# Linear attention and a token mixer in one kernel: the whole work list reordered, more value products on GpSimd

## The chip, the cores and the metric

The kernel runs on one core of one Trainium2 chip. The core has five engines that run their own instruction queues and meet only at semaphores: TensorE (PE in the profile; its weight loads are PEld), VectorE (DVE), ScalarE (ACT), GpSimd (POOL) and SyncE (SP), which here issues all transfers. Tiles lie in SBUF (128 partitions); matrix products land in PSUM (8 banks). The metric is the device time of one execution in microseconds (us), as the median of several runs.

## The reference

Inputs are q, k and v of shape (8 batches, 8 heads, 576 positions, 64 values) in float32, and three weight matrices. The first half is linear attention with position weights:

```python
theta = np.pi / 2.0 * pos / S
def phi(x, c, s):
    r = np.maximum(x, 0.0)
    return np.concatenate([r * c, r * s], axis=-1)
q_p = phi(q, cos_w, sin_w); k_p = phi(k, cos_w, sin_w)
kv = np.einsum('bhsf,bhsd->bhfd', k_p, v)
z = np.sum(k_p, axis=2)
num = np.einsum('bhsf,bhfd->bhsd', q_p, kv)
den = np.einsum('bhsf,bhf->bhs', q_p, z)[..., None] + 1e-06
```

num / den, with the heads side by side, is x of shape (8, 576, 512). The second half mixes tokens: wq = x @ w_q and wk = x @ w_k (512 to 64), W = wq wk^T / 8, mixed = W x, and the result is relu(mixed) @ w_out, of shape (8, 576, 512) in float32.

## The kernel before

The work is cut into 16 groups H of four heads (two for each batch b = H // 2), 8 batches, and 36 row tiles of the output. One string, ORDER, lists every step of the kernel as a short word, and a loop at the end of the kernel function turns the words into instructions one by one. A word is a kind, an index, an optional a or b (one half of a group), @A, @V or @G for ScalarE, VectorE or GpSimd, and :n for the PSUM bank or the slot of the output ring. Since each engine runs its own instructions in the order in which they were issued, ORDER fixes the queue of every engine; between engines only data and buffers decide. The scheduling is manual: nothing reorders the steps.

For a group H the steps are:

- LK, LQ, LV (line 145): half loads of k, q and v, 288 KB each, issued by SyncE into a ring of five float32 buffers (NRAW). LW loads weights, ST (line 519) stores a row tile.
- RK and RQ (lines 203 and 205): relu of k and q, float32 to bf16, on ScalarE, VectorE or GpSimd.
- The value products: v times the position weights vtab, twice as wide as v. Either CV casts v to bf16 and VS multiplies on VectorE (line 234), or VG multiplies on GpSimd straight from the float32 v (line 248). Both write v2, which has two buffers (NV2), so group H needs KV of group H - 2 done.
- KV (lines 275 and 285): k^T times v2 on TensorE; KE evicts it. For groups in KV_WIDE the product is taken in a wide form with 18 matmuls, else in 36 small ones.
- QT: transposes of q on TensorE, wide (line 295, 9 of 128 by 128) for groups in QT_WIDE, narrow (line 301, 18 of 64 by 64) else. QM (lines 316 and 320) multiplies the position weights onto them on VectorE, in two instructions for the wide form and one for the narrow one.
- N (line 340): numerators and denominators on TensorE, one step for each half group g = 2H, 2H + 1. For g in EPS_PE a small product adds the epsilon on TensorE (line 348); else EP adds it (lines 357 and 359). RC takes the reciprocal (line 378), RJ the same for two half groups at once (line 381). X multiplies (line 393) and writes x.
- XT or XR transposes x on TensorE (lines 406 and 419), XE evicts it.

For a batch: WK, WQ, KX (lines 439, 452, 466) with evictions KW, QW, XK and copies across partitions XA and XB; four MX (line 489) with ME (relu, lines 500 and 502). For each row tile: WO, four products with w_out (line 509), OE (eviction), ST (store). CW casts weights; the words that begin with T build tables and constants.

In the order before, stores stand among the last third of the loads in SyncE's queue; a store there waits until its row tile is evicted, and the loads behind it wait too.

The selection of one step's form, and the two ways to the products:

```python
def VS(H, ps, eng, part):
    V.tensor_mul(v2_b[H % NV2][:, part, :, :, 0:D],
        vb_b[H % NPREP][:, part].unsqueeze(3).to_broadcast([P, n, C, 2, D]), ...)
def VG(H, ps, eng, part):
        G.tensor_mul(dst[:, part, :, :, 0:D],
            s[:, part].unsqueeze(3).to_broadcast([P, n, C, 2, D]), ...)
```

Of the kernel before, what the change touches and what calls it, by code (L numbers as in the profile page):

```python
# [26 lines left out]
LK1b TB TI LQ1a LQ0a TK LV1b TZ LV1a LK1a LQ1b TQ LQ0b LK0a RQ1a@G LV0a TW TV LV0b LK0b CV1@A LV3a
LV3b VS1b RQ1b@A LQ3b VS1a T2 QT1:0 LQ3a RK1a@A RK1b@V RQ0@V LK3b KV1:2 QM1 LK3a QT0:4 KE1@A CV0@G
LV2b RK0@A LW1 N2:2 VS0 N3:0 LQ2a LK2a VG3 QM0 KV0:6 LW0 KE0@A LV2a RC3 EP2@A X3 RQ3@A N0:6 N1:4
LQ2b RC2 EP0@V EP1@V X2 RK3@A LK2b QT3:0 RC0 XT1:2 LV5b X0 LV5a XE1@A RC1 X1 VG2b KV3:6 QM3 LK5b  # L30
# [1 line left out]
RC6 LQ4a KX0:4 X6 RK2@A QT2:2 RC7 X7 CV5@A KV2:0 LK7a XK0@V LV4a QM2 XB0@G QW0@A XT3:6 LV4b KE2@A
RK5@A LK4a VS5a N5:0 WU5:2 LK4b N4:2 VS5b XE3@A RQ5@G LV7a EP5@V KV5:4 RC5 RC4 X5 XA0@A LV7b X4
QT5:6 KE5@A RQ4@G LQ7b MX0:0 QM5 XR2:2 ME0@A LQ7a QT4:4 XE2@A LQ6a N10:0 QM4 MX1:6 CV4@G LK7b EP10@A
ME1@A WK1:2 LV6b WQ1:3 RC10 KW1@A VS4 RK4@A LQ6b KX1:2 MX2:6 LW2 N11:4 XK1@V QW1@A ME2@A EP11@V
KV4:2 LK6b RC11 XA1@G X10 CV7a@A CV7b@G LK6a X11 MX5:6 MX4:0 KE4@A RQ7b@G LV6a RQ7a@A VS7 N8:2 N9:4
ME5@A LV8a ME4@A QT7:6 RK7@G LW3 EP8@V EP9@V RJ4 RQ6a@A XT5:0 X8 LW4 XB1@G XE5@A X9 KV7:2 LW5 RQ6b@G
QM7 LQ8b VG6b MX6:4 KE7@A XT4:0 LQ9b ME6@A MX7:2 XE4@V QT6:6 LV8b ME7@A N15:4 QM6 RK6a@A LQ8a MX3:2
N14:0 CV6a@G EP15@A RK6b@A WK2:6 LV9b ME3@A VS6a WQ2:7 LK8a KW2@A RC14 KV6:2 RC15 QW2@A LQ9a X14
CV8a@G KX2:7 LV9a KE6@A CW4@G X15 CW2@A N13:2 LK9a CW3@A CW5@V N12:0 EP13@V XR7:4 XK2@V LK8b WO8:6  # L40
RC13 XA2@A X13 EP12@A CV8b@G LK9b XE7@A WO2:7 RC12 VS8 LV11a WO7:2 CV9b@A RQ8a@G X12 OE8:0@A MX8:4
WO6:3 RQ8b@A RK8a@G LQ13a ME8@V OE7:1@A LQ11b XR6:0 RQ9a@G LQ10a WO1:6 CV9a@A XE6@V RQ9b@G LK11b
OE2:2@A WO4:2 LK11a VS9 OE6:3@A LQ11a RK8b@A QT9:0 RK9a@G OE1:4@A WK3:3 LV11b QM9 QT8:4 RK9b@G KW3@A
# [1 line left out]
WQ3:6 RC16 LQ10b KX3:7 X16 QW3@A MX10:0 LV10a XK3@A N17:4 ME10@A N19:2 RK11@V N18:6 LV10b EP19@A
WO11:0 EP17@V RQ11@A LQ12a RC17 EP18@V X17 WO5:1 VG11b OE11:6@V WO10:4 OE5:5@A RC19 RC18 ST11 X18
WO9:5 LK12a X19 LK10b QT11:6 LQ13b OE9:7@A RQ10@G LV12b KV11:2 XA3@A QM11 XR8:0 LK12b KE11@A XR9:6
VG10a XE8@A QT10:2 LQ12b XE9@V WO0:5 QM10 OE10:8@A MX13:0 OE0:6@A MX12:6 N22:2 WO12:4 RQ13a@G ME12@V
EP22@A LV15a XB3@A ME13@A LV13a RC22 VG10b WK4:5 X22 LQ14b LV14b MX14:0 KW4@A N23:6 ME14@V LQ14a
MX15:2 EP23@A KX4:5 RK10@A LV13b WQ4:0 XK4@V RQ13b@G RC23 WO3:1 ME15@A X23 XA4@G XB4@A QW4@A RQ12b@G  # L50
KV10:2 OE3:9@V RQ12a@A QT13:6 OE12:10@A VG12 MX18:0 WO14:5 QM13 KE10@A ST12 ME18@A LK13b XR11:2
OE14:11@A LK13a MX16:0 N21:6 XE11@V ME16@A LV14a N20:4 EP21@A EP20@V RK12@A QT12:0 RJ10 X21 WO16:2
RQ14b@A X20 WO13:3 QM12 VG13 XR10:4 OE13:10@A MX19:6 KV12:0 ME19@A ST13 WO17:3 OE16:12@A LK15b
KE12@V XE10@V LK14b MX17:0 LK14a OE17:13@A N25:6 ME17@V N24:4 LV15b RQ14a@A WK5:3 ST2 EP25@V EP24@V
RK13@A RJ12 QT14:0 X24 WO21:2 KW5@A X25 CV14a@G KV13:4 OE21:10@A QM14 CV14b@A WQ5:3 ST21 KE13@A
KX5:2 LQ15b VS14 LQ15a XR12:4 XK5@A N27:0 ST3 XE12@A N26:6 LK15a RK14a@G WO20:2 RC26 EP27@V RC27
XA5@G RK14b@A X27 WO19:4 XB5@G QW5@A VG15b X26 KV14:0 OE19:2@A MX21:6 KE14@A MX23:4 WO18:3 ME21@V
ME23@A OE20:10@V XR13:4 RQ15a@G MX22:6 RQ15b@V MX20:0 ST20 ME22@A WO15:2 VG15a ST17 XE13@V ME20@A
ST8 N28:6 OE18:9@V OE15:14@A ST9 N29:0 EP28@A QT15:4 RK15@A EP29@V RC28 WK6:3 RC29 X29 WO25:2 KW6@A
QM15 WQ6:3 OE25:15@A KV15:0 X28 QW6@A ST25 ST7 KX6:3 KE15@A ST15 N31:0 ST18 XR14:6 EP31@V N30:4 ST0  # L60
XE14@V WO23:2 EP30@A ST10 XK6@A RJ15 ST16 X30 XA6@G WO24:3 ST5 OE23:7@A XB6@G X31 WO26:2 OE24:0@A
ST14 XR15:0 ST6 MX25:4 MX27:6 XE15@V ME25@A WO22:3 ST23 ME27@V ST1 WK7:0 OE26:9@V ST24 MX24:6 KW7@A
MX26:4 WQ7:1 ME24@A ME26@V ST19 KX7:0 OE22:8@V ST26 WO28:2 XK7@A QW7@V ST22 XA7@G WO27:3 OE28:11@A
XB7@G ST28 MX31:0 MX28:4 MX30:6 ME31@V ME28@A WO29:2 ME30@A OE27:7@V MX29:4 OE29:4@V WO30:0 ME29@A
ST27 ST29 WO32:1 OE30:2@V WO33:4 ST30 OE32:9@V WO34:0 ST32 OE33:8@A WO35:1 ST33 OE34:7@V WO31:4 ST34
OE35:4@A ST35 OE31:2@A ST31
"""


# [1 line left out]
def kernel(  # L71
# [135 lines left out]
    def cast(eng, dst, s):  # L207
        if eng is A:
            A.copy(dst, s)  # L209
        elif eng is G:  # L210
            G.tensor_scalar(dst, s, 1.0, 1.0, op0=ALU.mult, op1=ALU.mult)  # L211
        else:
            V.tensor_copy(dst, s)  # L213
# [98 lines left out]
    def QM(H, ps, eng):
        if H in QT_WIDE:
            q_t = qt_wide(place["QT", H]).rearrange("p c (r d) -> p r c d", r=2)
            for r in range(2):
                V.tensor_mul(  # L316
                    qm_b[H % NQM][:, :, r, 0:C, :],
                    q_t[:, r].unsqueeze(1).to_broadcast([P, 2, C, H2]), qtab)
# [13 lines left out]
    def N(g, ps, eng):  # L332
# [3 lines left out]
        for u in range(SC):  # L336
            for s in range(2):
                for pr in range(2):
                    a = slice(H2 * pr, H2 * pr + H2)
                    nc.tensor.matmul(  # L340
                        nv[:, pr, u, :], qm_b[H % NQM][a, s, r, 2 * u:2 * u + 2, :],
                        kv_b[H % 2][a, r, pr if H in KV_WIDE else 0, s, 0:D + 1],
                        start=(u == 0 and s == 0),
                        stop=(u == SC - 1 and s == 1 and g not in EPS_PE))
# [254 lines left out]
```

## Time and profile before

| | |
|---|---|
| median of 3 runs | 120.03 us (119.75 to 120.36) |
| span of the profiled execution | 117.9 us, 4967 instructions (it is listed by its span alone) |
| busy in the span | PE 96.3, PEld 65.3, DVE 91.0, ACT 82.7, POOL 64.8 us |
| granted TensorE clock | 0.997 on the mean |
| moved by DMA | 39.38 MB, mean 334 GB/s |

The span runs from the first to the last instruction on the core. Busy time is the union of an engine's instructions. The rest of the runs' time lies around the span. The share of busy time is an average; the stretches of ten microseconds that are shown further down tell more.

### The profile page before, as it was taken

The page shows a single profiled execution, that of the slowest core. Times are in us where ns is not written, and L with a number is a line of the kernel's source. Part 1 is how long each engine was busy: PE and PEld are TensorE (multiplying, and loading weights), DVE is VectorE, ACT ScalarE, POOL GpSimd, SP SyncE. Part 2 cuts the span into 40 slices and gives each one's busy share as a digit, 9 for nine tenths or more (in the row PEclk, how much of TensorE's full clock was granted, in tenths as well). Part 3 has the DMA queues.
Part 4 walks back from the last instruction along what each step waited for, and adds up shares of the span by engine and source line. Part 5 has one row for each costly group of instructions (what it writes and reads, how often), then busy time and mean ns, then how long its engine had stood idle before and what let it go on. Part 6 is the DMA issues. An engine that isn't in the chain of part 4 may idle for free.

```text
span 117.9 us, 4967 instructions
## 1 busy us (share of the span) xinstructions
PE 96.3 (82%) x2109; PEld 65.3 (55%) x2109; DVE 91.0 (77%) x163; ACT 82.7 (70%) x146; POOL 64.8 (55%) x66
## 2 busy tenths in 40 slices
...
GB/s 95 353 389 408 393 363 351 391 389 396 385 393 389 391 385 387 389 395 384 387 381 341 271 317 379 274 253 215 299 285 321 171 205 268 402 343 402 340 306 172
DMA packets 20662, 39.38 MB, mean 334 GB/s; under 512 B 3232, under 2 KB 3232, under 8 KB 20640
## 3 DMA queue, kind: packets, MB, share of 16 engines
...
q8 instruction: 16, 0.26, 1.0%
...
## 4 chain that ended last, share of the span: by engine, by line
PE 46%; DMA 25%; DVE 9%; SPq 8%; ACT 4%; issue 3%; POOL 2%; POOLq 0%; DVEq 0%
PE ps L509 23%; DMA kraw<-in_k_dram 11%; DMA vraw<-in_v_dram 9%; SPq L145 8%; DMA qraw<-in_q_dram 5%; DVE qm L316 5%; PE ps L340 4%; PE ps L452 3%; PE ps L466 3%; PE ps L489 3%; PE ps L439 3%; PE ps L285 3%; PE ps L419 2%; PE ps L295 2%; POOL rq L205 2%
## 5 line engine op out<-in xcount | busy, mean ns | idle before, releaser
L248 POOL TENSOR_TENSOR v<-vraw,vtab 128x1152 bf16<-128x1152 f32 (+1 forms) x12 | 35.6, 2976 | 4.5 <-DVE qm L316 2.5
L509 PE MATMUL ps<-wow,mix 128*128 128x512 bf16 x144 | 34.6, 380 | 0.0
L393 DVE TENSOR_TENSOR x<-ps,rec 128x640 bf16<-128x640 f32 x32 | 25.4, 816 | 0.7
L209 ACT COPY o<-ps 128x512 f32<-128x512 f32 x25 | 14.6, 590 | 10.5 <-PE ps L509 9.2
L316 DVE TENSOR_TENSOR qm<-ps,qtab 128x1152 bf16<-128x1152 bf16 x28 | 19.7, 749 | 1.3 <-PE ps L295 1.2
L509 PEld LDWEIGHTS <-mix 128*128 128x128 bf16 x144 | 12.5, 98 | 14.5 <-issue 1.7
L295 PE MATMUL ps<-ident,rq 128*128 128x128 bf16 x126 | 10.3, 232 | 10.9 <-ACT rq L203 10.0
L234 DVE TENSOR_TENSOR v<-vb,vtab 128x2304 bf16<-128x2304 bf16 (+1 forms) x11 | 12.0, 1110 | 7.5 <-ACT vb L209 6.7
L500 ACT ACTIVATE mix<-ps 128x576 bf16<-128x576 f32 x23 | 14.5, 651 | 2.5 <-PE ps L489 2.3
L340 PE MATMUL ps<-kvs,qm 64*128 64x65 bf16 x640 | 14.0, 193 | 2.8 <-DVE qm L316 1.8
L340 PEld LDWEIGHTS <-qm 64*128 64x128 bf16 x640 | 12.6, 96 | 4.9 <-issue 3.3
L295 PEld LDWEIGHTS <-rq 128*128 128x128 bf16 x126 | 8.2, 104 | 12.5 <-issue 9.9
L203 ACT ACTIVATE rk<-kraw 128x1152 bf16<-128x1152 f32 (+1 forms) x14 | 13.9, 995 | 0.5 <-DMA kraw<-in_k_dram 0.3
L211 POOL TENSOR_SCALAR kx<-kx 64x256 bf16<-64x256 bf16 x10 | 4.0, 400 | 15.8 <-ACT kx L209 10.1
L205 POOL TENSOR_SCALAR rq<-qraw 128x576 bf16<-128x576 f32 (+1 forms) x13 | 10.1, 776 | 4.4 <-ACT rk L203 2.6
L211 POOL TENSOR_SCALAR vb<-vraw 128x576 bf16<-128x576 f32 (+1 forms) x7 | 5.7, 809 | 10.8 <-DMA vraw<-in_v_dram 9.5
L285 PE MATMUL ps<-v,rk 64*64 64x130 bf16 x432 | 9.1, 228 | 1.9 <-ACT mix L500 0.7
L209 ACT CAST kvs<-ps 128x260 bf16<-128x260 f32 (+1 forms) x15 | 6.5, 436 | 5.1 <-PE ps L285 3.8
L285 PEld LDWEIGHTS <-rk 64*64 64x64 bf16 x432 | 7.5, 112 | 4.3 <-ACT mix L500 1.3
L502 DVE TENSOR_SCALAR mix<-ps 128x576 bf16<-128x576 f32 x9 | 6.8, 753 | 3.3 <-PE ps L489 3.1
L213 DVE COPY xT<-ps 128x1280 bf16<-128x1280 bf16 (+1 forms) x9 | 7.3, 813 | 2.2 <-PE ps L419 2.0
L203 ACT ACTIVATE rq<-qraw 128x576 bf16<-128x576 f32 (+1 forms) x10 | 8.3, 830 | 0.9 <-DMA qraw<-in_q_dram 0.8
...
## 6 DMA issues: line engine op xcount, KB each, us to landing
...
```

What stands on the lines that cost most here:

```text
L203: A.activation(dst, s, AF.Relu)
L205: eng.tensor_scalar(dst, s, FMAX, 0.0, op0=ALU.min, op1=ALU.max)
L209: A.copy(dst, s)
L234: V.tensor_mul(v2_b[H % NV2][:, part, :, :, 0:D], vb_b[H % NPREP][:, part].unsqueeze(3).to_broadcast([P, n, C, 2, D]), vtab.unsqueeze(1).t ...
L248: G.tensor_mul(dst[:, part, :, :, 0:D], s[:, part].unsqueeze(3).to_broadcast([P, n, C, 2, D]), vtab.unsqueeze(1).to_broadcast([P, n, C, 2, ...
L285: nc.tensor.matmul(kv_v[o, r, :], rk_of(H)[a, pr, c, :], v2_b[H % NV2][a, pr, c, :, 0:D + 1], start=(c == 0), stop=(c == C - 1))
L295: nc.tensor.transpose(qt_v[:, c, :], rq_b[H % NPREP][:, c, :, :], ident)
L316: V.tensor_mul(qm_b[H % NQM][:, :, r, 0:C, :], q_t[:, r].unsqueeze(1).to_broadcast([P, 2, C, H2]), qtab)
L340: nc.tensor.matmul(nv[:, pr, u, :], qm_b[H % NQM][a, s, r, 2 * u:2 * u + 2, :], kv_b[H % 2][a, r, pr if H in KV_WIDE else 0, s, 0:D + 1], ...
L393: V.tensor_tensor(x_b[b % NX][:, :, 4 * h:4 * h + 4, :].rearrange("p u (w r) d -> p r w u d", r=2)[:, r], nv[:, :, :, 0:D], rec(g).to_broa ...
L500: A.activation(dst, s, AF.Relu, scale=scale_moe)
L509: nc.tensor.matmul(o, mix_b[bp % 2][:, m, rt * P:(rt + 1) * P], wow[:, m, :], start=(m == 0), stop=(m == NDM - 1))
```

## The change

ORDER is written anew from end to end, and four selections change. What can be counted in the two orders:

| | before | after |
|---|---|---|
| value products on GpSimd (VG) | 9 halves, 3 full | 18 halves, 3 full |
| value products on VectorE (VS) | 5 halves, 6 full | 4 halves, 2 full |
| relu of k and q on GpSimd | 14 halves, 4 full | 6 halves, 4 full |
| casts of v on GpSimd | 5 halves, 2 full | 2 halves |
| copies XA and XB on GpSimd | 10 | 3 |
| QT in the wide form | 14 of 16 | 4 of 16 |
| KV in the wide form | 4 of 16 | 0 |
| half groups with epsilon on TensorE | 5 | 10 |
| reciprocals RC / joint RJ | 24 / 4 | 32 / 0 |
| evictions OE on ScalarE / VectorE | 25 / 11 | 21 / 15 |
| evictions ME on ScalarE / VectorE | 23 / 9 | 26 / 6 |
| evictions XE on ScalarE / VectorE | 7 / 9 | 5 / 11 |

The one warm-up product WU is gone, and the first stores stand later in the list. [...] The core of the diff, with the part of the new order from the first stage to KV8 and the end of the loads:

```diff
 ORDER = """
...
-XR0:4 KE3@A CW1@A N6:0 LK5a LQ5a XE0@V EP6@A N7:6 CW0@G LQ5b EP7@A WK0:4 VG2a RQ2@A LQ4b WQ0:5 KW0@V
...
-OE4:5@A KV8:0 QM8 XB2@A KV9:6 ST4 KE8@A LV12a MX9:4 KE9@A MX11:0 VG11a N16:2 ME9@A LK10a ME11@V
...
+TZ TK TQ LQ1a LV1b LV1a LK1a TV CV1b@V T2 VS1b LV0b LK1b LQ0a CV1a@A TW LV0a CV0a@A LQ1b LV3b VS1a
+RK1a@V LQ0b RQ1a@V TB LK0b RK1b@A RQ1b@V TI QT1:0 KV1:2 LK0a LK3b LW1 RQ0a@A LQ3b RQ0b@A CV0b@V VS0
...
+RK5b@A XE2@V QM5 LK6b LK6a MX0:2 MX3:0 CV4b@G CV4a@G WQ1:4 WK1:5 KW1@A ME0@A RQ4@V KV5:6 LW5 KE5@A
+KX1:5 XK1@A VS4 XB1@A RK4@A ME3@A LW4 QW1@V N11:6 LV8a QT4:2 EP11@V KV4:4 RC11 LW3 VG7a VG7b QM4
+XA1@A MX7:0 KE4@A X11 ME7@A N10:2 MX4:4 VG6b RC10 LQ8a ME4@A N8:6 VG6a RK7a@A N9:0 LV9b X10 MX2:4
+LQ8b MX5:2 RC8 RK7b@A RC9 LQ9a LQ9b X8 LV9a X9 XT5:6 XR4:0 ME2@A MX6:4 ME5@A RQ7@A XE5@V KV7:2
+RQ6a@A XE4@V QT7:6 WK2:0 KE7@V RK6a@G RQ6b@A LK9b WQ2:1 LK9a KW2@A CW2@G CW4@G ME6@A QT6:2 QM7 LV8b
+RK6b@A QM6 N15:6 RC15 KX2:0 LK8b LV10a LK8a KV6:4 CW5@G VG8a LV11a VG9b VG9a N14:2 KE6@A N13:4 X15
+XK2@V LQ11a N12:6 EP14@A CW3@A EP12@A WO5:0 RC13 QW2@A XA2@A RC14 X13 WO2:1 OE5:0@A RC12 LQ11b VG8b
+LV11b WO4:0 X12 X14 RQ8@A XB2@A OE4:1@A XR6:2 XR7:6 OE2:2@V QT8:4 WO1:1 XE6@V WO8:0 RQ9@A QT9:2
+XE7@V OE1:3@A RK9b@A MX10:6 WK3:1 RK9a@A ME10@A QM8 QM9 KV9:4 KW3@A OE8:4@V MX9:2 MX8:6 LK11b KX3:1
+KE9@A LK11a ME8@V LV10b ME9@A N19:4 MX11:6 RK8@G LK10a EP19@V LQ10b LQ10a ME11@A CV11a@A LK10b N18:2
+XK3@V EP18@V WO10:0 LV13a RC19 LK13a XA3@A RC18 KV8:6 OE10:5@A KE8@A WQ3:1 X19 N16:6 N17:4 VS11a
...
+LQ15a MX19:6 WQ5:4 KX5:5 ST6 RC27 EP25@V RQ14a@G RC25 ME19@A X27 X25 RQ14b@G QW5@A LK15b LK15a N24:6
+XK5@A XR13:0 XB5@A EP24@V MX18:4 VG14 RC24 WO13:2 X24 ME18@A WO17:3 ST15 OE13:2@A XE13@V XR12:6
+MX22:0 XA5@A RQ15@A QT14:4 WO21:2 XE12@V WK6:6 ME22@A WO18:7 QM14 OE17:1@A MX21:4 OE21:0@A KW6@A
+MX23:2 RK14@A MX20:0 ST17 OE18:8@V ST16 ME23@A WQ6:6 RK15@G ME21@V KX6:7 QW6@V ME20@V XK6@V KV14:4
+KE14@A KV15:2 QT15:0 ST21 N28:6 N29:4 QM15 KE15@A WO23:2 WO25:3 WO19:0 EP28@A EP29@A RC28 RC29 X28
...
 """
...
-    EPS_PE = (3, 4, 14, 16, 26)
+    EPS_PE = (0, 1, 2, 4, 6, 8, 9, 10, 13, 15)
...
-    QT_WIDE = (0, 1, 2, 3, 4, 5, 6, 7, 8, 9, 10, 11, 12, 14)
-    KV_WIDE = (2, 4, 5, 7)
+    QT_WIDE = (0, 1, 2, 3)
+    KV_WIDE = ()
```

More of the change, by code (lines that the diff above doesn't have):

```diff
@@ L26 @@
 ORDER = """
[L27 to L30, printed above, removed]
-XR0:4 KE3@A CW1@A N6:0 LK5a LQ5a XE0@V EP6@A N7:6 CW0@G LQ5b EP7@A WK0:4 VG2a RQ2@A LQ4b WQ0:5 KW0@V
@@ L32 @@
[L32 to L43, printed above, removed]
@@ L44 @@
-OE4:5@A KV8:0 QM8 XB2@A KV9:6 ST4 KE8@A LV12a MX9:4 KE9@A MX11:0 VG11a N16:2 ME9@A LK10a ME11@V
[L45 to L66, printed above, removed]
+TZ TK TQ LQ1a LV1b LV1a LK1a TV CV1b@V T2 VS1b LV0b LK1b LQ0a CV1a@A TW LV0a CV0a@A LQ1b LV3b VS1a
```

22 lines of the change are left out of this document (added).

## The prediction

> **What bounds the kernel now.** I read the spans and the busy time by stretch first, then the chain that ended last, then TensorE, GpSimd and VectorE in order of time.
>
> ```profile
> core 0: 117.9 us, clock 0.997
> ...
> 10.00:20.00 10.00, 8.19 (x241) 6.95 (x241) 9.18 (x19) 6.11 (x9) 6.96 (x3) 1.00 1.07 375
> 20.00:30.00 10.00, 7.95 (x199) 6.07 (x192) 9.02 (x18) 7.71 (x13) 5.55 (x5) 1.00 1.06 391
> ...
> 50.00:60.00 10.00, 9.49 (x235) 6.82 (x235) 8.66 (x13) 8.29 (x18) 6.60 (x7) 1.00 1.05 388
> 60.00:70.00 10.00, 9.11 (x172) 5.47 (x165) 8.50 (x18) 6.47 (x13) 9.27 (x6) 1.00 0.97 323
> 70.00:80.00 10.00, 9.86 (x228) 6.29 (x226) 8.49 (x14) 8.83 (x18) 7.16 (x5) 1.00 0.88 303
> 80.00:90.00 10.00, 9.33 (x243) 6.42 (x247) 8.72 (x17) 7.57 (x14) 6.76 (x6) 1.00 0.86 280
> 90.00:100.00 10.00, 10.00 (x274) 6.39 (x274) 8.15 (x16) 6.68 (x14) 5.17 (x4) 1.00 0.61 218
> ```
>
> The columns after the length are busy us of PE, PEld, DVE, ACT and POOL, then granted clock, DMA share and GB/s. Up to 60 us the DMA engines are full (share 1.05 to 1.07) and PE idles up to 2 us in ten; a load of 288 KB at 391 GB/s enters every 0.754 us (294,912 bytes / 391). From 60 us on the DMA share falls and PE idles 0.89 + 0.14 + 0.67 us in the next thirty, then nothing. So the kernel has two stages: inputs set the pace at first, TensorE's remaining work sets the end. The chain says the same of its last part:
>
> ```profile
> 77.05 0.66 PE ps L295 x9
> ...
> 93.59 0.72 PE ps L340 x40
> 94.31 0.26 PE ps L301 x18
> ...
> 96.74 0.65 PE ps L285 x35
> 97.39 0.67 PE ps L466 x10
> ...
> 107.31 0.47 PE ps L489 x6
> ...
> 108.98 5.30 PE ps L509 x24
> 114.28 0.02 issue
> 114.30 0.58 ACT o L209
> ```
>
> The last matmul ends at 108.98 + 5.30 = 114.28, and 117.9 - 114.3 = 3.6 us follow for the last eviction and its store. The prices are here too: a query transpose QT in the wide form costs 0.66, in the narrow form 0.26; one N 0.36 (0.72 for two), one KV 0.65, one KX 0.67, one MX 0.16 (0.47 for three).
>
> So the question for the new order is one of time and rest: when does TensorE reach the dense stage, and how much is then left? TensorE takes its steps in the written order, so a good mark is a step that both orders have at its entrance. I take KV8, with these rows of TensorE's timeline:
>
> ```profile
> 33.80 0.74 PE L466 MATMUL ps<-x,wk 128*64 128x256 bf16 x10
> ...
> 45.47 0.72 PE L285 MATMUL ps<-v,rk 64*64 64x130 bf16 x36
> ...
> 56.01 1.25 PE L285 MATMUL ps<-v,rk 64*64 64x130 bf16 x72 [0.43 <-DVE qm L316]
> ```
>
> They are KX1, KV6, and KV8 with KV9. From KV8's start to the last matmul the kernel before needs 114.28 - 56.01 = 58.3 us, its idle time included.
>
> **The change part by part: the work that is left.** I counted the steps from KV8 on in both orders. Before: 30 WO, 23 MX, 16 N, 8 KV, 8 XR, 6 QT (4 of them wide), 5 WQ, 5 KX, 4 WK. After: 30 WO, 20 MX, 14 N, 7 KV, 8 XR, 6 QT (all narrow), 5 WQ, 4 KX, 4 WK. The new order has therefore done 3 MX (0.47), 2 N (0.72), 1 KV (0.65) and 1 KX (0.67) earlier, and saves 4 x (0.66 - 0.26) = 1.6 on the transposes: 4.1 us less. What KV_WIDE = () saves lies ahead of KV8. So 58.3 - 4.1 = 54.2 us are left, if the idle time stays what it was.
>
> **When KV8 starts.** KV8 needs the products of v for pair 8 and RK8, and both now come from GpSimd. Half products on GpSimd go from 9 (with 3 full ones) to 18 (with 3 full ones). The rows of GpSimd, in order of time:
>
> ```profile
> 38.35 1.15 POOL L205 TENSOR_SCALAR rk<-kraw 128x1152 bf16<-128x1152 f32 x1 [1.09 <-ACT mix L500]
> ...
> 40.69 2.37 POOL L248 TENSOR_TENSOR v<-vraw,vtab 128x1152 bf16<-128x1152 f32 x1
> ...
> 45.52 0.62 POOL L211 TENSOR_SCALAR wow<-wof 128x512 bf16<-128x512 f32 x1
> ...
> 47.61 0.68 POOL L211 TENSOR_SCALAR vb<-vraw 128x576 bf16<-128x576 f32 x1 [1.47 <-DMA vraw<-in_v_dram]
> ...
> 49.94 0.91 POOL L205 TENSOR_SCALAR rk<-kraw 128x576 bf16<-128x576 f32 x1 [0.82 <-DMA kraw<-in_k_dram]
> ...
> 53.61 1.21 POOL L205 TENSOR_SCALAR rk<-kraw 128x576 bf16<-128x576 f32 x1 [0.87 <-DMA kraw<-in_k_dram]
> ...
> 57.36 5.22 POOL L248 TENSOR_TENSOR v<-vraw,vtab 128x1152 bf16<-128x1152 f32 x2 [2.54 <-DVE qm L316]
> ...
> 66.24 0.67 POOL L205 TENSOR_SCALAR rq<-qraw 128x576 bf16<-128x576 f32 x1
> 66.87 2.38 POOL L248 TENSOR_TENSOR v<-vraw,vtab 128x1152 bf16<-128x1152 f32 x1
> ```
>
> The GpSimd queue after, between KV5 and KV8, is: VG7a VG7b VG6b VG6a RK6a CW2 CW4 CW5 VG8a VG9b VG9a VG8b RK8. VG7 waits for KV5, which frees the buffer of v2. In the new order KV5 stands just ahead of KX1; the old KX1 began at 33.80, on the same loads (the last of pair 2 is SP's 25th issue instead of the 26th), so I let KV5 end at 33.8. VS4 on VectorE may come in between, since VectorE and GpSimd shut each other out (below): 0 to 1.4 us, of which I take half. From 34.5 on: 8 half products x 2.37 = 19.0, RK6a 0.67, three casts x 0.62 = 1.9, RK8 1.15, together 22.7, so GpSimd is done at 57.2. Its inputs are there: V8b is SP's 64th issue instead of the 58th, 6 x 0.754 = 4.5 us later than the 47.61 at which the old cast was released, 52.1 against VG8b's start at 53.7; K8a moves from 61st to 67th, 49.94 + 4.5 = 54.4 against RK8's 56.1. RK6a ends at 44.7 and frees KV6 when the old order ran it (45.47). I add 0.3 for TensorE's WO10 just ahead of KV8: KV8 starts at 57.5, 1.5 us later than before. Its bounds are 56.0 (the old time) and 61.5 (every product held up by the lock, the slower rival below).
>
> **What the exclusion is worth by itself.** These rows of VectorE stand beside those of GpSimd:
>
> ```profile
> 40.44 1.41 DVE L316 TENSOR_TENSOR qm<-ps,qtab 128x1152 bf16<-128x1152 bf16 x2
> 41.93 0.76 DVE L213 COPY xT<-ps 128x1152 bf16<-128x1152 bf16 x1
> ...
> 52.95 1.35 DVE L234 TENSOR_TENSOR v<-vb,vtab 128x2304 bf16<-128x2304 bf16 x1
> ...
> 59.53 0.82 DVE L205 TENSOR_SCALAR rk<-kraw 128x1152 bf16<-128x1152 f32 x1
> ```
>
> VS9 holds VectorE from 52.95 to 54.30. GpSimd's RK9b, begun at 53.61, takes 1.21 instead of the 0.67 of its size and ends 0.5 after VS9: it stood still for the overlap. The pair of products at 57.36 takes 5.22 instead of 2 x 2.37 = 4.74, with RK11 on VectorE inside it. QM7 and XE4, which read PSUM, run beside the product at 40.69, and none is slower. [...] I count no gain for it.
>
> [...]
>
> ```profile
> L248 POOL TENSOR_TENSOR v<-vraw,vtab 128x1152 bf16<-128x1152 f32 x9 | 21.9, 2433 | 3.0 <-DVE qm L316 2.5 <-DMA vraw<-in_v_dram 0.4
> ...
> L234 DVE TENSOR_TENSOR v<-vb,vtab 128x1152 bf16<-128x1152 bf16 x5 | 3.6, 754 | 6.8 <-ACT vb L209 6.7
> ```
>
> **Edits costed at nothing.** The joint reciprocals (RJ) become eight single ones, five more denominators get their epsilon on TensorE, and evictions change places between VectorE and ScalarE: a few tenths each, on engines that are 60 to 92% busy in the stretches above. If that cover fails on VectorE in the first stage (9.18 of 10 us busy), KV8 moves by the same tenths. QT1 comes behind the 9th load, not the 7th: 1.5 us later at the start, hidden because TensorE idles about 2 us of every ten there and waits for loads; without that cover it costs 1.5. The stores stand later in SP's queue: the last load is the 106th issue with 4 stores ahead of it instead of the 109th with 7. After it 32 stores of 256 KB at 0.67 us (262,144 bytes / 391 GB/s), 21.4 us, have to pass. The load can issue at about 102 x 0.754 + 4 x 0.67 = 80, so the stores could end near 102, ahead of 114; each us by which the loads are later than 92 would show at the end.
>
> **GpSimd after KV8.** RQ11, VG11b, VG10b, then VG13 behind KV11, VG12, RQ12, VG15, RQ14, VG14 and RK15: 10 halves' worth is 23.7, the rest 1.15 + 1.15 + 1.33 + 1.15 = 4.8. With about 2.5 of waiting for KV11 (which stands some 7 us of TensorE's work behind KV8) it ends at 57.2 + 31 = 88.2. TensorE's order from KV15 on holds 16 WO (5.30 / 6 = 0.88 each, 14.1), 8 MX, 4 N, KV15, QT15, KX7 and four smaller steps, 20.5 us in all, so it comes to KV15 near 57.5 + 54.2 - 20.5 = 91.2. GpSimd is some 3 us ahead: covered, but not by much.
>
> **The sum.** 57.5 + 54.2 + 3.6 = 115.3 us of span against 117.9. The profiled execution is listed by its span alone; the median of the runs, 120.03, is 2.1 longer, so I add 2.1: 117.4 us.
>
> **The rivals.** (a) GpSimd is no limit at KV8, which starts at the old 56.0 on the same loads: 117.4 - 1.5 = 115.9. For it speaks that old KV8 waited only for QM on VectorE; against it the 22.7 us of GpSimd's queue.
>
> (b) No change. The 4.1 us that TensorE saves are spent waiting for KV8: the whole of VS4 in front of VG7 (+0.7), RQ4 on VectorE too (+0.8), and KX1's projections, WO10 and the evictions before it each a little late (+1): KV8 at 60.0, 119.9. For it speaks that all gains sit in TensorE, which idles in the first stage anyway.
>
> (c) Slower. VectorE holds GpSimd at every product from KV5 to KV8, as RK11 did once: 5.22 - 4.74 = 0.5 us at a meeting (RK9b lost 1.21 - 0.67 = 0.5 as well). Eight products lose 4.0, the casts behind them start that much later, KV8 moves to 61.5 and TensorE, in its written order, stands before it: 117.4 + 4.0 = 121.4. It decides (slower by over 0.5%) once GpSimd loses more than 3.2 us in that stretch. [...]
>
> **How the numbers follow.** Chances: 0.50 for 117.4, 0.15 for (a), 0.17 for (b), 0.18 for (c). Half a per cent, 0.6 us, is about what a measurement of this kernel tells from no change: faster is below 119.4, slower above 120.6. That gives 0.65, 0.17 and 0.18. The range runs from 115.2, a little under (a), to 121.2, which is (c) without its worst. The likeliest case alone spans 116.0 to 119.2, KV8 from 56.1 to 59.3.
>
> **What would show it.** QT in the narrow form at about 0.26 to 0.33 and no wide KV. The KV8 row at 57.5, released by GpSimd's rk or v; if it is released by something else, the GpSimd sum is wrong. From KV8 on 54 us to the last matmul with about 2 us idle; more idle, released by GpSimd's v or rk, means that its lead of 3 us was not there. Products of 2.4 us throughout; many near 2.9 would be (c). I am wrong in kind if PE is not dense after 60 us, or if the last stores are what ends the span more than 4 us after the last matmul.

## The result and the profile after

The changed kernel is slower: 125.58 us as the median of four executions (124.57 to 126.38) against 120.06 for the kernel before on the same chip, a ratio of 1.044 (95% interval 1.038 to 1.050). The prediction was 117.4 with 115.2 to 121.2 as its range, so it missed the time by 8.2 us and had the sign wrong. (Medians here are over all executions of a kernel; ratios leave out single executions far above the fastest ones.) The profiled execution of the changed kernel took 124.57 us, with a span of 122.7.

The busy time by stretch of the changed kernel, with the columns of the prediction's first fence:

```profile
core 0: 122.7 us, clock 0.984
...
30.00:40.00 10.00, 6.62 (x239) 5.18 (x236) 7.82 (x13) 7.16 (x14) 8.47 (x6) 1.00 1.05 389
40.00:50.00 10.00, 6.78 (x231) 5.19 (x227) 8.22 (x13) 6.51 (x12) 6.55 (x6) 1.00 1.05 388
50.00:60.00 10.00, 10.00 (x229) 6.10 (x221) 7.30 (x11) 8.06 (x16) 9.46 (x5) 0.83 1.05 391
...
90.00:100.00 10.00, 10.00 (x240) 6.34 (x236) 8.17 (x15) 7.70 (x15) 6.56 (x5) 1.00 0.51 192
```

The loss sits between 30 and 60 us. TensorE is busy 6.62 and 6.78 us of ten there, and from 50 to 60, where it looks full, its granted clock is 0.83 on the mean. The last stretch shown is as dense as before. GpSimd's queue in order of time shows the same stretch from the other side:

```profile
33.98 10.13 POOL L248 TENSOR_TENSOR v<-vraw,vtab 128x1152 bf16<-128x1152 f32 x4 [1.45 <-PE ps L285]
...
44.93 1.78 POOL L211 TENSOR_SCALAR wow<-wof 128x512 bf16<-128x512 f32 x3
50.45 9.39 POOL L248 TENSOR_TENSOR v<-vraw,vtab 128x1152 bf16<-128x1152 f32 x4 [3.74 <-issue]
```

Its products and casts run on time as far as 44.93 + 1.78 = 46.71. Then GpSimd stands idle for 3.74 us: VG8a writes the buffer of v2 that KV6 reads, and KV6 is late (it ends at 50.31, VG8a begins at 50.45, though the row names no releaser but "issue"). TensorE's own order of time says why:

```profile
36.58 0.71 PE L285 MATMUL ps<-v,rk 64*64 64x130 bf16 x33 [1.32 <-ACT rk L203]
38.76 0.25 PE L285 MATMUL ps<-v,rk 64*64 64x130 bf16 x3 [1.47 <-issue]
...
42.98 0.48 PE L285 MATMUL ps<-v,rk 64*64 64x130 bf16 x19
44.13 0.47 PE L285 MATMUL ps<-v,rk 64*64 64x130 bf16 x17 [0.67 <-issue]
44.54 0.44 PE L301 MATMUL ps<-ident,rq 64*128 64x64 bf16 x18
44.91 0.76 PE L439 MATMUL ps<-wkw,xT 128*128 128x64 bf16 x20
45.59 0.68 PE L452 MATMUL ps<-xT,wqw 128*64 128x288 bf16 x8
46.21 0.44 PE L301 MATMUL ps<-ident,rq 64*128 64x64 bf16 x18
46.48 0.47 PE L340 MATMUL ps<-kvs,qm 64*128 64x65 bf16 x20
46.79 0.17 PE L348 MATMUL ps<-epsr,ones 64*128 64x5 bf16 x2
46.89 0.74 PE L466 MATMUL ps<-x,wk 128*64 128x256 bf16 x10
47.56 0.42 PE L285 MATMUL ps<-v,rk 64*64 64x130 bf16 x15
49.78 0.53 PE L285 MATMUL ps<-v,rk 64*64 64x130 bf16 x21 [1.80 <-issue]
...
52.08 3.63 PE L509 MATMUL ps<-wow,mix 128*128 128x512 bf16 x12
...
63.16 0.72 PE L285 MATMUL ps<-v,rk 64*64 64x130 bf16 x36
```

KV4, KV7 and KV6 stop in the middle of their 36 matmuls, after 33, 19 and 15 of them, for 1.47, 0.67 and 1.80 us, although the operands of all 36 are the same tiles. The releaser is "issue": nothing that the profile shows was waited for. The counts of the rows tell where TensorE stops. From the standstill in KV7 to the one in KV6 lie 17 + 18 + 20 + 8 + 18 + 20 + 2 + 10 + 15 = 128 matmuls, each with its own weight load: 256 instructions. From KV4's to KV7's there are again 128. (A row here is one instruction of TensorE, a matmul or a weight load.) Counted over the whole trace, with TensorE's few semaphore instructions, these stops stand at rows 1216, 1472 and 1728, and the next stop inside a KV, at 83.64 us, at row 3264: every one a multiple of 256 behind the first. The prediction's mark, KV8, starts at 63.16 instead of 57.5. In the chain of waits the twelve WO matmuls there take 3.56 us; twelve at 98.98, at full clock, take 2.70. The clock's record shows half speed (0.50 granted) from 50.5 to 53.9 us, right after KV6's standstill.

Part 3 of the page counts the transfers that bring instructions, first in the kernel before, then in the changed one (packets, MB, share of 16 engines):

```profile
q8 instruction: 16, 0.26, 1.0%
```

```profile
q8 instruction: 18, 0.29, 1.0%
```

0.26 MB in 16 packets is 16 KB a packet, and two more of them came with 5288 - 4967 = 321 more instructions. In the trace's transfers, packets of that queue begin at 36.2, 41.6 and 47.3 us, and TensorE goes on at 38.76, 44.13 and 49.78, some 2.5 us behind each. In the kernel before the packets begin in similar steps of 5.7 to 7.6 us (29.4, 35.0, 40.8, 48.4), but there TensorE never stands for them by more than 0.25 us. So this is the first reading, theory I, to be tested: TensorE gets its instructions in blocks of 256, as the steps of the rows suggest; at a DMA share of 1.05 a block takes some 5.5 us from the entry into the block before it to its own use (44.13 - 38.76 = 5.4, 49.78 - 44.13 = 5.6); and an order that uses up 256 rows faster than that stands still. The narrow forms of QT and KV have twice the rows of the wide ones: TensorE has 2320 rows ahead of KV8 instead of 1858.

### The profile page after: what moved, and what is told of

It reads as the page before. It is cut to its first block, busy times and chain, and to the rows that moved or that the text cites. A ratio compares the mean times of both kernels' runs of the same rounds, so it can differ in the third digit from the quotient of the medians.

```text
span 122.7 us, 5288 instructions
## 1 busy us (share of the span) xinstructions
PE 94.1 (77%) x2280; PEld 62.2 (51%) x2280; DVE 91.1 (74%) x161; ACT 80.8 (66%) x150; POOL 73.4 (60%) x56
## 4 chain that ended last, share of the span: by engine, by line
PE 52%; DVE 16%; DMA 15%; issue 6%; ACT 5%; SPq 2%; DVEq 0%; ACTq 0%
PE ps L509 24%; DMA qraw<-in_q_dram 10%; PE ps L285 6%; PE ps L340 5%; DMA wkf<-in_moe_w_k_dram 5%; DVE x L393 4%; DVE qm L320 3%; PE ps L439 3%; PE ps L419 3%; PE ps L466 3%; DVE v L234 3%; PE ps L489 3%; PE ps L452 3%; PE ps L301 2%; SPq L145 2%
## 5 line engine op out<-in xcount | busy, mean ns | idle before, releaser
L248 POOL TENSOR_TENSOR v<-vraw,vtab 128x1152 bf16<-128x1152 f32 (+1 forms) x21 | 57.3, 2747 | 13.6 <-PE ps L285 8.0
L509 PE MATMUL ps<-wow,mix 128*128 128x512 bf16 x144 | 35.1, 388 | 0.0
L509 PEld LDWEIGHTS <-mix 128*128 128x128 bf16 x144 | 12.8, 99 | 15.4 <-issue 1.8
L320 DVE TENSOR_TENSOR qm<-ps,qtab 128x2304 bf16<-128x2304 bf16 x12 | 16.1, 1348 | 1.5 <-PE ps L301 1.5
L203 ACT ACTIVATE rk<-kraw 128x576 bf16<-128x576 f32 (+1 forms) x20 | 15.2, 784 | 1.6 <-DMA kraw<-in_k_dram 1.5
L213 DVE COPY o<-ps 128x512 f32<-128x512 f32 x15 | 10.3, 690 | 4.4 <-PE ps L509 4.2
L295 PE MATMUL ps<-ident,rq 128*128 128x128 bf16 x36 | 3.6, 266 | 12.1 <-DVE rq L205 11.6
L209 ACT CAST kvs<-ps 128x260 bf16<-128x260 f32 x13 | 4.9, 378 | 10.9 <-PE ps L285 8.9
L205 POOL TENSOR_SCALAR rk<-kraw 128x576 bf16<-128x576 f32 (+1 forms) x5 | 4.4, 887 | 9.1 <-DMA kraw<-in_k_dram 8.9
L489 PE MATMUL ps<-wq,kx 64*128 64x288 bf16 x64 | 8.1, 285 | 1.2 <-DVE x L393 0.5
L295 PEld LDWEIGHTS <-rq 128*128 128x128 bf16 x36 | 2.8, 120 | 12.4 <-DVE rq L205 11.6
L234 DVE TENSOR_TENSOR v<-vb,vtab 128x1152 bf16<-128x1152 bf16 (+1 forms) x6 | 6.7, 1114 | 0.7 <-ACT vb L209 0.5
```

What stands on the lines that cost most here:

```text
L203: A.activation(dst, s, AF.Relu)
L234: V.tensor_mul(v2_b[H % NV2][:, part, :, :, 0:D], vb_b[H % NPREP][:, part].unsqueeze(3).to_broadcast([P, n, C, 2, D]), vtab.unsqueeze(1).t ...
L248: G.tensor_mul(dst[:, part, :, :, 0:D], s[:, part].unsqueeze(3).to_broadcast([P, n, C, 2, D]), vtab.unsqueeze(1).to_broadcast([P, n, C, 2, ...
L320: V.tensor_mul(qm_b[H % NQM][:, :, :, 0:C, :].rearrange("p s r c d -> p s r (c d)"), qt_view(place["QT", H]).unsqueeze(1).to_broadcast([P, ...
L489: nc.tensor.matmul(pair(ps)[:, t, :].bitcast(FP32)[:, 0:HS], kx_b[b % 2][a, (m // 2) ^ t, (m % 2) * P:(m % 2 + 1) * P], wq_b[b % 2][a, :], ...
L509: nc.tensor.matmul(o, mix_b[bp % 2][:, m, rt * P:(rt + 1) * P], wow[:, m, :], start=(m == 0), stop=(m == NDM - 1))
```

## The experiments

The other readings: G, that GpSimd with its 18 half products is what comes too late at KV8 while the narrow forms save what the prediction gave them; O, that the written order has particular steps too late in front of KV4 and KV8. Two more, K and F, stand with their runs.

**The form lists by themselves, in either order.** First the new order with the old lists:

```diff
-    QT_WIDE = (0, 1, 2, 3)
-    KV_WIDE = ()
+    QT_WIDE = (0, 1, 2, 3, 4, 5, 6, 7, 8, 9, 10, 11, 12, 14)
+    KV_WIDE = (2, 4, 5, 7)
```

> The new order with the old forms: QT_WIDE and KV_WIDE as before the change. Theory I (instruction supply): TensorE's instructions arrive in blocks of 256 over the same DMA engines as the loads; while these are full, a block is there only some 5.4 us after TensorE entered the block ahead of it (after: entered at 38.76, 44.13, 49.78). Ahead of KV8 this kernel has 2068 TensorE instructions instead of 2320, one block less. The standstills inside KV4, KV7 and KV6 (1.47, 0.67 and 1.80 us) go or shrink to under 1.5 in all, KV8 starts at 58 to 60 instead of 63.16, four wide QT behind it cost 1.6: 121 to 122.5 us. Theory G (GpSimd is late with its products of v, whatever TensorE's form): KV8 stays at 63 and the time is 125.6 + 1.6 = 127.

Measured: 122.16 us (121.49 to 124.43), ratio to the kernel before 1.016 (1.009 to 1.023). GpSimd's queue and, in a fence of their own, TensorE's rows in this kernel:

```profile
35.19 9.70 POOL L248 TENSOR_TENSOR v<-vraw,vtab 128x1152 bf16<-128x1152 f32 x4 [2.55 <-PE ps L275]
...
45.72 1.78 POOL L211 TENSOR_SCALAR wow<-wof 128x512 bf16<-128x512 f32 x3
48.49 9.38 POOL L248 TENSOR_TENSOR v<-vraw,vtab 128x1152 bf16<-128x1152 f32 x4 [0.99 <-POOL wow L211]
57.95 1.15 POOL L205 TENSOR_SCALAR rk<-kraw 128x1152 bf16<-128x1152 f32 x1
```

```profile
47.61 0.72 PE L285 MATMUL ps<-v,rk 64*64 64x130 bf16 x36
...
60.35 0.72 PE L285 MATMUL ps<-v,rk 64*64 64x130 bf16 x36
...
63.77 0.19 PE L340 MATMUL ps<-kvs,qm 64*128 64x65 bf16 x1 [1.24 <-issue]
```

KV6 runs in one piece, GpSimd's wait for it falls from 3.74 to 0.99 (the row names the cast ahead, but that had ended at 47.50, and KV6 at 48.33), KV8 comes at 60.35, and the record of the clock has no half-speed stretch until the end. One standstill is left behind KV8. So 125.58 - 122.16 = 3.4 us of the loss is that of the narrow forms, which were to save; 1.6% stays with the order. (A second measurement of the changed kernel, further down, makes it less.)

Then the opposite, the old order with the new lists:

```diff
-    QT_WIDE = (0, 1, 2, 3, 4, 5, 6, 7, 8, 9, 10, 11, 12, 14)
-    KV_WIDE = (2, 4, 5, 7)
+    QT_WIDE = (0, 1, 2, 3)
+    KV_WIDE = ()
```

> The old order with the new forms: QT narrow from group 4 on, no wide KV. GpSimd and the order are the old ones. Theory I: 2110 TensorE instructions ahead of KV8 instead of 1858; standstills without a releaser appear at rows 256 apart, between 25 and 55 us, KV8 starts at 58 to 60 instead of 56.0, four narrow QT behind it give back 1.6: 121.5 to 124 us. Theory G: the GpSimd queue is unchanged, TensorE has less work: 118 to 118.6 us.

Measured: ratio 1.026 (1.017 to 1.034), some 3.1 us by the 120.37 us of the kernel before, measured beside it; the median of all four executions is 124.92. They took 122.44, 124.18, 125.65 and 129.07 us, at mean granted clocks of 1.000, 0.980, 0.972 and 0.941; the third is the profiled one (span 123.9). From its TensorE's order of time:

```profile
42.06 0.59 PE L285 MATMUL ps<-v,rk 64*64 64x130 bf16 x26 [0.99 <-DVE x L393]
43.45 0.54 PE L285 MATMUL ps<-v,rk 64*64 64x130 bf16 x10 [0.80 <-issue]
...
49.09 0.72 PE L285 MATMUL ps<-v,rk 64*64 64x130 bf16 x36
...
59.49 0.72 PE L285 MATMUL ps<-v,rk 64*64 64x130 bf16 x36 [0.39 <-DVE qm L320]
```

KV6 at 49.09 was at 45.47 before, KV8 at 59.49 was at 56.01. Half clock stands in the record from 32.8 to 36.3 and from 43.1 to 46.5 (0.83 on the mean of 30 to 40 and of 40 to 50 us), so part of these 3.5 us is the clock's; the execution at full clock lost 122.44 - 120.37 = 2.1 us. The lists alone, with no step moved and no product moved to GpSimd, slow the old order too: G is no account of this half.

**Narrow only where the loads are over.** If the form saves TensorE's time once blocks come fast, the narrow QT should pay late. Two runs, the new order with the early groups wide, and the old order with the late QT narrow:

```diff
-    QT_WIDE = (0, 1, 2, 3)
-    KV_WIDE = ()
+    QT_WIDE = (0, 1, 2, 3, 4, 5, 6, 7, 8, 9)
+    KV_WIDE = (2, 4, 5, 7)
```

> The new order with the wide QT for groups 0 to 9 and the old wide KV (2, 4, 5, 7), narrow QT from group 10 on: few instructions while the DMA engines are full, little TensorE work afterwards. Theory I: as the one with all old forms up to KV8 (58 to 60), and 1.6 us less behind it: 119.5 to 121 us. Theory G: 125.6 as after the change.

```diff
-    QT_WIDE = (0, 1, 2, 3, 4, 5, 6, 7, 8, 9, 10, 11, 12, 14)
+    QT_WIDE = (0, 1, 2, 3, 4, 5, 6, 7, 8, 9)
```

> The old order, QT narrow for groups 10, 11, 12 and 14 as well, nothing else. Both theories: no instruction is added ahead of KV8, 4 x 0.4 = 1.6 us of TensorE work go from the dense stage: 118.2 to 118.8 us. If the narrow form itself were what costs, it would be over 120.5.

Measured: the first 122.07 (121.81 to 122.73), ratio 1.016 (1.011 to 1.021), no better than e1; the second 120.5 over 12 executions, ratio 1.0015 (0.998 to 1.005), no change. Both expectations missed, and with them my price. The stretch from KV8 to the last matmul, in the kernel before and in this one:

```profile
56.00:114.00 58.00, 56.21 (x1180) 34.70 (x1179) 46.55 (x80) 39.25 (x75) 32.41 (x22) 1.00 0.87 308
```

```profile
56.00:114.00 58.00, 54.69 (x1204) 33.78 (x1215) 46.25 (x76) 38.96 (x74) 32.18 (x22) 1.00 0.86 307
```

TensorE's busy time falls by 1.5 us (56.21 to 54.69), but that is too much: 13 of the 144 WO matmuls of e4 have no record in its trace, and a missing one reads as a stop of about 0.2 us "for issue" in front of L509. Without L509 the fall is 30.51 to 29.72, 0.8 us or 0.2 a step. Of this little arrives, since the last matmul ends at 114.09 instead of 114.26. Step against step, e4 leads by 0.10 us at KV8 (55.91 against 56.01) and by 0.50 at 89.43, and 0.33 of it goes in the KV that begins there: behind its fifth weight load TensorE stands for 0.27 us with no releaser, at a step of 256 rows, 2.4 us behind a block's packet at 87.4. So by this stop the blocks took 0.27 us back in this stage too, at a share of 0.80 (86 to 96 us); the rest of the lead goes in waits of a few tenths for VectorE's qm and ScalarE's mix.

**Room on the DMA engines.** Theory I says that blocks are late because loads fill the DMA engines. So both orders without the loads of k, relu of k reading the q buffer instead, every computing step kept:

```diff
+        if nm == "k":
+            return
...
-        relu(eng, rk_of(H)[:, part], raw["k"][H % NRAW].rearrange("p r (c d) -> p r c d", d=D)[:, part])
+        relu(eng, rk_of(H)[:, part], raw["q"][H % NRAW].rearrange("p r (c d) -> p r c d", d=D)[:, part])
```

> The old kernel without the loads of k: RK reads the raw q in its place, so a third of the q, k, v loads is gone and the numbers for k are wrong; all computing stays. Both theories: a base for its twin. Inputs stop being the pace after the ring is filled (some 20 us); DMA share falls under 0.9 from then on; time 112 to 118 us.

> The new kernel without the loads of k (RK reads the raw q, the numbers for k are wrong, all computing stays). Theory I (instruction blocks wait behind the loads): with the DMA engines no longer full, a block is there about 3.5 to 4 us after the one ahead of it was entered instead of 5.4, the standstills without a releaser between 30 and 55 us are gone, TensorE's clock keeps its full rate, and the ratio to the twin falls from 1.044 to 1.00 to 1.02 (what is left is the order's own). A rival (the narrow forms or the order cost the same whatever the DMA engines do): the ratio stays at 1.04 or more.

Measured: the old order 124.75 us, ratio 1.041 (1.033 to 1.049); the new order 116.28 (114.74 to 124.30), ratio to the kernel before 0.958 (0.952 to 0.964). The old order became slower with less to load. In its profile one product of VectorE stands beside a full product of GpSimd (GpSimd's row, then VectorE's; the lines of this kernel stand 2 later):

```profile
11.50 4.54 POOL L250 TENSOR_TENSOR v<-vraw,vtab 128x2304 bf16<-128x2304 f32 x1
```

```profile
11.77 5.48 DVE L236 TENSOR_TENSOR v<-vb,vtab 128x2304 bf16<-128x2304 bf16 x1
```

It took 5.48 us instead of the 1.35 of VS9; TensorE stood 3.92 us for it, and half clock from 17.1 to 24.0 followed (0.86 and 0.80 on the mean of 10 to 20 and 20 to 30 us). Whether that is the whole of the loss is not shown: two of the other executions lost about as much (123.92 and 124.91 us) at a mean clock of 1.000. So this run is no base for the other, and their ratio of 0.93 decides nothing between the theories. What the second shows by itself is where standstills are left. Its busy time by stretch:

```profile
30.00:40.00 10.00, 7.55 (x256) 6.06 (x254) 8.95 (x16) 8.25 (x17) 7.73 (x3) 1.00 0.98 357
40.00:50.00 10.00, 9.43 (x304) 6.63 (x298) 9.05 (x16) 8.17 (x16) 9.57 (x8) 1.00 0.68 221
```

In KV4 and KV7 TensorE stops at the same 33rd and 19th matmul, for 0.36 and 0.40 us; the share was still 0.99 from 37 to 39 us, ahead of KV7's stop at 40.64. KV6, from 44.47 on, runs in one piece: its block was entered 3.6 us behind the one before. GpSimd's VG8a starts at 45.34 after 0.26 us of waiting. So in this run, at a share of 0.98 from 30 to 40 us and 0.68 from 40 to 50, the three stops are 0.36, 0.40 and 0 us instead of 1.47, 0.67 and 1.80 at 1.05; how much of the 9 us against the changed kernel is due to blocks and how much to the loads that are gone, this run can't part.

**Particular steps too late (O), and GpSimd's share (G).** Both runs start from e3. The first moves RK4 ahead of three steps on ScalarE and KV8 ahead of WO10; the second gives group 8's half products back to VectorE, with casts on ScalarE:

```diff
-... ME0@A RQ4@V KV5:6 LW5 KE5@A KX1:5 XK1@A VS4 XB1@A RK4@A ME3@A ...
+... ME0@A RK4@A RQ4@V KV5:6 LW5 KE5@A KX1:5 XK1@A VS4 XB1@A ME3@A ...
...
-XK3@V EP18@V WO10:0 LV13a RC19 LK13a XA3@A RC18 KV8:6 OE10:5@A ...
+XK3@V EP18@V LV13a RC19 LK13a XA3@A RC18 KV8:6 WO10:0 OE10:5@A ...
```

> The new order with wide forms for the early groups (122.07 us), and two steps moved: RK4 on ScalarE ahead of KE5, XK1 and XB1, and KV8 on TensorE ahead of WO10. Theory O (the order itself makes KV4 and KV8 wait in line behind steps that are late): KV4 starts 1 to 1.5 us earlier (37.0 instead of 38.4), KV8 1.5 to 2 earlier, the time falls by 1 to 2: 120.2 to 121.2 us. Theory G (GpSimd's queue sets KV8): RK8 ends where it did (near 59.5), KV8 gains only the 0.8 of WO10, and the time falls by under 0.8.

```diff
-... KV6:4 CW5@G VG8a LV11a VG9b VG9a ... RC12 LQ11b VG8b
+... KV6:4 CW5@G CV8a@A VS8a LV11a VG9b VG9a ... RC12 LQ11b CV8b@A VS8b
```

> The new order with wide forms for the early groups (122.07 us), and the two halves of v of group 8 cast on ScalarE and multiplied on VectorE instead of GpSimd, so that GpSimd's queue up to RK8 is 4.7 us shorter. Theory G (GpSimd's queue sets KV8): RK8 ends 3 to 4 us earlier, KV8 starts at 58 or before instead of 61.0, and the time falls by 1.5 to 3. Theory O (TensorE and ScalarE come to KV8 late on their own): KV8 moves by under 1 us and the time by under 0.8.

Measured: 122.58 (ratio 1.021, 1.016 to 1.026) and 127.64 (1.064, 1.059 to 1.069), neither a gain. In the first, KV4 did move from 38.37 to 37.48 and KV8 from 61.0 to 60.15, about the 0.8 that theory G expected, and TensorE waits 0.43 us for GpSimd there. The end did not gain, and the trace shows where the lead went:

```profile
75.49 0.81 PE L509 MATMUL ps<-wow,mix 128*128 128x512 bf16 x3 [1.13 <-issue]
...
85.22 0.73 PE L340 MATMUL ps<-kvs,qm 64*128 64x65 bf16 x35 [0.60 <-issue]
```

As far as 73 us this kernel leads e3 by 0.64 us. The same two stops are 0.35 and 0.32 us long in e3, and they lie on the steps of 256 rows (the first to within a missing record): the blocks took back 0.78 and 0.28 us. So these two steps are worth nothing here, but the run doesn't show that no step of the order is too late. In the second, GpSimd's RK8 and VectorE's two products read:

```profile
56.60 1.51 POOL L205 TENSOR_SCALAR rk<-kraw 128x1152 bf16<-128x1152 f32 x1 [2.15 <-DMA kraw<-in_k_dram]
```

```profile
49.43 2.79 DVE L234 TENSOR_TENSOR v<-vb,vtab 128x1152 bf16<-128x1152 bf16 x1 [1.03 <-PE ps L285]
...
56.35 0.76 DVE L234 TENSOR_TENSOR v<-vb,vtab 128x1152 bf16<-128x1152 bf16 x1 [1.96 <-ACT vb L209]
```

GpSimd ended only 1.6 us earlier (58.1 instead of 59.7), because RK8 now waited for the load of k. VectorE paid more: VS8a, a form that takes 0.754 on the mean in the kernel before (L234 in the prediction's rows), stood 2.79 beside a product on GpSimd, and VS8b waited 1.96 for ScalarE's cast. TensorE stood 2.71 us for x; behind that, from 53.42, five WO matmuls took 2.13 us where seven take 1.90 from 59.84 (the execution's mean clock was 0.982), and KV8 came at 66.60. So the moved products are not a loss that can be undone alone; the run says nothing on what GpSimd costs otherwise.

**Moving the blocks' boundaries.** Here 64 tiny matmuls ahead of QT1 shift all later rows by 128, half a block. Measured beside it are the changed kernel itself and e1 padded to the changed kernel's rows:

```diff
+    def blank(n, ps):
+        for _ in range(n):
+            nc.tensor.matmul(bank(ps)[0:H2, 0:8], wc[0:H2, WARM_COLS:WARM_COLS + H2],
+                             wc[0:H2, 0:8], start=True, stop=True)
...
         place["QT", H] = ps
+        if H == 1:
+            blank(64, ps)
```

> The changed kernel with 64 tiny matmuls (64 by 64 weights, 8 columns, into a bank that the next step overwrites) ahead of QT1, where TensorE waits for loads: 128 rows of TensorE more, half of a step of 256, ahead of everything. Theory I (instruction supply in blocks of 256 rows): the standstills leave the middles of KV4, KV7 and KV6 and come half a block earlier in the list, inside N11, inside N9 and at the start of QT6, and half a block behind KV6, near the first WO; as the list is the same and only its phase moves, the time stays within 1.5 us of the changed kernel, 123.5 to 126.5. Rival K (the standstills belong to these three KV steps, through a wait on rk or v2 that the profile does not name): they stay at the 33rd, 19th and 15th matmul of KV4, KV7 and KV6 and keep their 1.5, 0.7 and 1.8 us.

```diff
         place["QT", H] = ps
+        if H in QT_WIDE and H > 3:
+            blank(9, ps)
...
         if H in KV_WIDE:
+            blank(18, ps)
```

> The changed kernel with the wide forms of the kernel before, each padded by tiny matmuls (9 ahead of a wide QT other than 0 to 3, 18 ahead of a wide KV; 8 columns, into a bank that the step overwrites): the wide forms' work, but as many rows of TensorE at every step as in the changed kernel. Without the padding it measured 122.2 with KV8 at 60.35. Theory I (the number of rows decides): standstills of TensorE inside or at KV4, KV7 and KV6 again, KV8 back at 62 to 63.5, 124 to 126.5 us. Rival F (the narrow forms are slower by themselves, their count of rows being no matter): KV8 at 60.3 to 61, since the tiny matmuls take 0.1 to 0.25 us a step and stand in a stage that waits for loads, and 122.2 to 123.2 us.

> The changed kernel itself once more, as the base of the two runs beside it: 124.6 to 126.4 us as measured first, standstills of TensorE inside KV4, KV7 and KV6, KV8 near 63.

Measured: the shifted kernel 129.8 (ratio 1.077, 1.068 to 1.086), the padded one 128.08 (1.062, 1.058 to 1.067), the changed kernel again 124.9 (1.034, 1.027 to 1.040). TensorE's order of time in the shifted kernel, whose lines stand 7 later:

```profile
9.14 3.57 PE L292 MATMUL ps<-warm 64*64 64x8 bf16 x64 [9.14 <-DVE warm L546]
...
40.08 0.37 PE L347 MATMUL ps<-kvs,qm 64*128 64x65 bf16 x13
41.85 0.29 PE L347 MATMUL ps<-kvs,qm 64*128 64x65 bf16 x7 [1.39 <-issue]
...
45.26 1.15 PE L285 MATMUL ps<-v,rk 64*64 64x130 bf16 x36
...
49.39 0.72 PE L285 MATMUL ps<-v,rk 64*64 64x130 bf16 x36
...
50.98 0.19 PE L347 MATMUL ps<-kvs,qm 64*128 64x65 bf16 x1
52.60 0.48 PE L347 MATMUL ps<-kvs,qm 64*128 64x65 bf16 x19 [1.42 <-issue]
```

KV4, KV7 (45.26) and KV6 (49.39) run in one piece now, and the standstills lie inside N9, as expected, and inside an N behind KV6, 512 rows later; at QT6 and N11 there was none. Counted as above, the two stops stand at rows 1472 and 1984 of this kernel, on the same steps of 256 as in the changed kernel, though the list is shifted by 128. And in these two profiles, in e2, in e6 and in the second profile below, TensorE goes on 2.3 to 2.6 us behind the start of a block's packet at each of eleven stops on these steps of 256. The KV steps had nothing to do with it: K falls, and theory I's places hold. Its time does not: I had put the tiny matmuls into idle time, but they took 3.57 us, the first QT starts at 12.65 instead of 11.58, and four stretches of half clock follow (22.3, 42.8, 53.1, 77.0; 0.83 to 0.85 on the mean of their ten us). The padded kernel tells nothing apart, and its 128.08 us fit neither reading: nine tiny matmuls took 0.44 us and eighteen 0.70, all 162 together 7.3, and TensorE, busied by them, stood for no releaser only once ahead of KV8, which came at 64.78. So F is not tested by this run; against it speak the shorter busy times of the narrow steps (below) and the grid of 256.

In the changed kernel's second profile TensorE's rows read:

```profile
38.01 0.25 PE L285 MATMUL ps<-v,rk 64*64 64x130 bf16 x3 [0.79 <-issue]
...
48.20 0.53 PE L285 MATMUL ps<-v,rk 64*64 64x130 bf16 x21 [1.16 <-issue]
...
60.63 0.72 PE L285 MATMUL ps<-v,rk 64*64 64x130 bf16 x36
...
65.29 0.54 PE L419 MATMUL ps<-ident,x 64*128 64x64 bf16 x18 [0.73 <-issue]
```

The places are the same rows, the lengths are not, and KV7 has no stop here. Half clock stands in the record from 38.2 to 41.6 (0.91 and 0.92 on the mean of 30 to 40 and 40 to 50 us). KV8 comes 2.5 us earlier than in the first profile, but a standstill and a second stretch of half clock (65.5 to 68.9; 0.83 on the mean of 60 to 70) lie behind it, and the last matmul ends at 117.92 as it did at 117.96. By this measurement the lists cost less: 1.034 against the 1.016 of e1 is 2.1 us.

## Why the prediction was wrong

**The step that failed most: the edits costed at nothing.** The two form lists were priced by TensorE's time alone, four QT by 0.4 for -1.6 us, and for KV_WIDE = () the text only said that its saving lies ahead of KV8. That the narrow forms hold twice the instructions, and what supplies these, was no term of the sum. e1 against the changed kernel measures the lists at +3.4 us (+2.1 with the changed kernel's second measurement), e2 at +3.1 (2.0 to 4.1) in the old order. What the runs show in place of the saving are the stops of TensorE at every 256 rows, 1.47 + 0.67 + 1.80 us ahead of KV8, and the half clock behind them. Against the -1.6 of the sum the 3.4 are 5.0 of the 8.2 us.

**The price of QT was off too.** The 0.26 was a short piece of the chain. The groups say 5.3 us for 12 narrow QT, 0.44 each, in the changed kernel, and 10.4 for 14 wide ones, 0.74, in e1:

```profile
L301 PE MATMUL ps<-ident,rq 64*128 64x64 bf16 x216 | 5.3, 191 | 0.0
```

```profile
L295 PE MATMUL ps<-ident,rq 128*128 128x128 bf16 x126 | 10.4, 233 | 11.5 <-DVE rq L205 11.1 <-DVE rec L378 0.4
```

That is 0.30 a step instead of 0.4; e4 saved 0.2 a step in busy time, and hardly any of it reached the end.

**KV8 at 57.5.** In the changed kernel 63.16 and 60.63; in e1, without the standstills in KV4, KV7 and KV6, 60.35. These 2.85 us are the order's own: VG7a begins at 35.19 instead of 34.5 (KV5 is the wide one there, 1.19 us long); VG8a waits 0.99 for KV6, which ran at 47.61 and not at 45.47, because TensorE's own list puts WK2, WQ2, QT6, N15 and KX2 in front of it, while the sum let it run as soon as RK6a was done; and KV8 follows RK8's end, 59.1, by 1.25 instead of 0.3, behind TensorE's steps. GpSimd's sum itself held: the casts ended at 46.7 in the changed kernel (46.5 by the prediction's rows), and eight products took 19.5 us (19.0).

**What was left from KV8.** 54.2 was right where nothing disturbed it: 117.96 - 63.16 = 54.8 in the first profile. In e1 it was 115.89 - 60.35 = 55.5 against 54.2 + 1.6 for the wide QT; but these 55.5 hold a standstill of 1.24 us, which no term foresaw, so that the agreement is partly luck. The second profile has 57.3 with 0.7 of standstill and a 3.4 us stretch of half clock in it; by the twelve WO matmuls of the first profile, which lost 3.56 - 2.70 = 0.86 us in the 1.8 that they ran at half clock, such a stretch costs some 1.6 us, an estimate.

**The tail.** The span ends 122.7 - 117.96 = 4.7 us after the last matmul, not 3.6; a store takes 3.7 us from issue to landing on the median, and 32 of them stand in one run of SP's queue, from 85.60 on. The prediction named more than 4 us as a sign that the last stores end the span. The sign was there, but it is only 1.1 us of the miss; e1 has 119.7 - 115.89 = 3.8.

Added up for the order alone: 117.4 + 1.6 (old forms) + 2.85 (KV8) = 121.85, against 122.16 measured in e1. With +3.4 for the lists this is the changed kernel as measured first. How these 3.4 divide between standstills and half clock stays open: no profile with all loads had the narrow lists without half clock, and the lengths differ between executions of one kernel. In the old order the one execution at a mean clock of 1.000 still lost 2.1 us (e2). Rival (c) had slower at 121.4, but its mechanism didn't act: products took 2.44 on the mean, and the first four 10.13 instead of 9.5, one meeting with VS4. In the changed kernel the exclusion was worth little, as the prediction counted. But the price of half a us at a meeting was too low in two other runs: VectorE's products took 2.79 instead of 0.754 in e9 and 5.48 instead of 1.35 in the old order without k, where GpSimd's product had begun first. That a relu of q on VectorE holds GpSimd up as well (RQ4, the 0.8 of rival (b)), no run shows: in the kernel before, GpSimd's half relu at 92.06 took its usual 0.67 us beside VectorE's RQ (0.74 from 92.20), and the product behind it, from 92.69, 2.38. The sign "PE not dense after 60 us" wasn't there; the harm was done before.
